# A searched order with an offset for each kind of operation, and scores of the global queries taken over each key once

## The chip, the cores and the metric

The kernel runs on 1 core of one Trainium2 chip. The metric is the device time of one execution in microseconds, in the median of several runs. A profiled execution has a time of its own and, a little shorter, a span from its first to its last instruction; stretches and sums below are of that span.

## The reference

Three stages follow each other, for 4 batches of 576 tokens. The first is an attention of 8 heads in which 32 global queries see all 544 keys, and 512 local queries see the 32 global keys and the local keys at a distance of at most 32. The second is a causal attention with 4 experts, of which a gate picks two for each token. The third is a convolution of three taps with a gate.

```python
s_g = scale * q_g @ concat(k_g, k_l).T          # 32 x 544, every key once
out_g = softmax(s_g) @ concat(v_g, v_l)
out_l = softmax(concat(q_l @ k_g.T, band(q_l @ k_l.T, 32))) @ concat(v_g, v_l)
x = concat(out_g, out_l) as (B, 544, 512)
logits = x @ w_gate; w = softmax over the two largest
out = sum over experts e: w_e * (causal_softmax(x@wq[e], x@wk[e]) @ (x@wv[e])) @ wo[e]
h = relu(out @ w_in); y = (h * sigmoid(conv3(h))) @ w_out
```

The second stage works on 544 tokens here, with inputs in float32; `w_in` is folded with `wo` into one matrix before it is used.

## The kernel before

The work is divided into some 1,900 operations (`op`), each a small group of instructions of one engine with a tag, for example `scoresA` (TensorE) or `expA` (ScalarE). The program doesn't issue them in the order in which it is written. `Schedule.run` places them one after the other: on each engine, among the operations whose inputs are ready, it takes the one with the smallest priority `prio`. A priority is a due time: `at(kind, b, f)` sets it from the table `PLAN` (stage A, B or C of batch b, and the weights' stages F, U, W) and the fractions in `SUB`. `HOLD` is added on TensorE to the priority of an operation that needs the array in another tile shape than the last, `HORIZON` says how far ahead of the earliest open due time an operation may be taken, and `CAPS` how many buffers of a kind may live at once. All engines then run their instructions in the order that came out, and SyncE (SP) issues all loads and stores in its order; a later instruction of an engine never passes an earlier one that waits.

Stage A of a batch (`stage_a`) treats two head pairs at a time. `local` does one head pair: masked scores on TensorE with the array in tiles of 64x32 (L550, L558; tag `scoresA`, 64 records), their maximum on VectorE (L561), 8 exponentials on ScalarE (L567), 8 transposes (L574, array whole) with a copy after each four (L576), the product with V in tiles of 128x32 (L587), its normalisation on VectorE (L594 to L596), 4 transposes (L604), and the copy into the buffer X, as a rounded part on ScalarE (L606) and a rest on VectorE (L361). `glob` does the 32 global queries of two head pairs: scores (L618), maximum (L622), one exponential (L624), 6 transposes (L633), product with V (L646), one transpose (L666), copies into X (L681). The keys are laid out in 24 blocks of 32 (`key_blocks`), in which the global keys stand six times, so that each local query block finds its keys in one run of 128; the global queries' scores run over 22 of the blocks, 704 columns, and `zG` clears the repeated blocks afterwards.

Stage B (`stage_b`) needs all of X of a batch: projections L708 (q, k) and L728 (v and gate), then for each of four query tiles i scores in tiles of 64x128 (L788, L793; two head pairs), exponentials (L800), transposes (L806), the product with V (L816 or L824) and a transpose (L837). Stage C is L919 (first matrix) and L957 (second), 12 matmuls each, 32 and 64 such blocks, with relu, convolution and gate between them on ScalarE, VectorE and GpSimd. The weights are prepared on the chip: `split_weights` (L432, L358), `decode` of `w_in` and `w_out` (L460 to L470), and `fold` (L493, L494), 8 blocks. Result blocks leave by L961 on ScalarE and the store L963.

Of the kernel before, what the change touches and what calls it, by code (L numbers as in the profile page):

```python
# [148 lines left out]
class Schedule:  # L149
# [1 line left out]
    LAT = {"PE": 0.04, "ACT": 0.055, "DVE": 0.055, "POOL": 0.05, "SP": 0.0}  # L151
    TAIL = {"PE": 0.17, "ACT": 0.1, "DVE": 0.06, "POOL": 0.03}
    SWITCH = 0.15
    SLACK = 0.063
    HOLD = 0.47
    HORIZON = 56.132
    RATE = 415e3
    SHARED = {"wi", "wu", "guard", "gate", "cv", "gt", "scB", "cwc"}

    def __init__(self):  # L160
# [3 lines left out]
    def op(self, eng, dur, fn, r=(), w=(), g=(), mode=None, size=0, lead=0.0, tag=""):  # L164
        o = Op()
        o.eng, o.dur, o.fn, o.mode, o.size, o.tag = eng, dur, fn, mode, size, tag
        o.prio = self.prio - lead
        o.port = "DVE" if eng == "POOL" else "POOL" if eng == "DVE" and tag in self.SHARED else None
        o.n = len(self.ops)
        o.succ, o.wait, o.ready = [], 0, 0.0  # L170
        before, bufs = {}, {}
        for t in r:
            wr, rd = self.last.setdefault(t, ([], []))
            before.update(dict.fromkeys(wr))
        for t in w:
            wr, rd = self.last.setdefault(t, ([], []))
            before.update(dict.fromkeys(wr))
            before.update(dict.fromkeys(rd))
        for t in g:
            wr, rd = self.last.setdefault(t, ([], []))  # L180
            before.update(dict.fromkeys(wr))
            before.update(dict.fromkeys(rd))
        for t in w:
            self.last[t] = ([o], [])
        for t in r:
            if t not in w:
                self.last[t][1].append(o)
        for t in tuple(r) + tuple(w):
            b = t[0] if isinstance(t, tuple) else t
            if isinstance(b, Buf):  # L190
                bufs[b] = 1
        o.bufs = tuple(bufs)
        for b in bufs:
            b.left += 1
        for p in before:
            p.succ.append(o)
            o.wait += 1
        self.ops.append(o)
        return o

    def run(self, trace=None):
# [8 lines left out]
        while left:  # L210
# [48 lines left out]
            elif o.eng == "SP":  # L259
                free["SP"] = t + 0.45  # L260
                dma = max(dma, t + 1.6) + o.size / self.RATE
                end = dma + 0.9
            else:
                if o.port:
                    t = max(t, port[o.port])
# [32 lines left out]
def t_pool(n, two=False):  # L298
    return (200 + (2.1 if two else 1.05) * n) * 1e-3


PLAN = {"A": [(-9.1, 23.2), (27.9, 79.0), (79.4, 165.8), (164.7, 245.1)],
        "B": [(34.0, 82.4), (87.3, 167.4), (178.8, 261.8), (257.7, 331.7)],
        "C": [(92.3, 184.6), (173.0, 288.4), (267.5, 353.2), (351.8, 398.6)],
        "F": (29.4, 53.5),
        "U": (62.9, 102.6),
        "W": (18.7, 72.1)}


CAPS = dict(raw=1, t=2, p=2, P=6, PT=2, PU=5, hb=4, cv=3, Pg=1, PGT=1)  # L310

MEM = (13, 9, 3, 4, 14)

SUB = {"lk": 15.574, "lv": 8.685, "ly": 7.388, "lw": 9.802, "ag": 0.054, "az": 0.179, "bq": 0.033, "bp": 0.145, "bv0": 0.113,
       "bv": 0.03, "bg": 0.301, "b0": 0.264, "b1": 0.436, "b2": 0.674, "b3": 0.738, "bl": 0.688, "bs": 0.012, "ch": 0.08,
       "co": 0.252, "cm": 0.179, "cf": 0.034, "cz": 0.549, "pi": 0.0, "pu": 0.0}


@with_exitstack
def body(ctx, tc, kq, vA, wqv, woT, w_in, conv_w, w_out, cmask, out, trace=None,  # L320
# [221 lines left out]
    def local(b, kb, v0, v1, X):  # L542
# [63 lines left out]
        op("ACT", t_act(512, 1), lambda: act.activation(X.ap()[:, 32:S], tx.ap(), AF.Copy), r=[tx], w=[(X, "h")], tag="xh")  # L606
        op("DVE", t_dve(512), lambda: sub(X.ap()[:, S + 32:2 * S], tx.ap(), X.ap()[:, 32:S]), r=[tx, (X, "h")], w=[(X, "l")], tag="xl")

    def glob(b, u, kqs, vs, X):
        G = PB(2, 3)  # L610

        def scores():
            for a, e in ((0, 512), (512, 704)):
                for z in range(2):
                    for y in range(2):
                        rows = slice(64 * y, 64 * y + 64)
                        c = 2 * z + y
                        pe.matmul(G.ap()[32 * c:32 * c + 32, a:e], kqs[z].ap()[rows, KB + 512:KB + 544], kqs[z].ap()[rows, a:e],  # L618
                                  start=True, stop=True)
        op("PE", 1.17, scores, r=[kqs[0], kqs[1]], w=[G], mode="64x32", tag="scoresG")  # L620
        st, Pg, PGT = ST(), W(2, 4, "Pg"), W(2, 0, "PGT")
        op("DVE", t_dve(704), lambda: dve.tensor_reduce(st.ap()[:, 0:1], G.ap()[:, :704], axis=AX.X, op=ALU.max, negate=True), r=[G], w=[st], tag="maxG")  # L622
        op("POOL", .25, lambda: scale_pool(st.ap()[:, 1:2], st.ap()[:, 0:1], 0.125), r=[st], w=[(st, 1)], tag="sclG")
        op("ACT", t_act(704, 1, 1), lambda: act.activation(Pg.ap()[:, :704], G.ap()[:, :704], AF.Exp, bias=st.ap()[:, 1:2], scale=0.125),  # L624
           r=[G, (st, 1)], w=[Pg], tag="expG")
        op("POOL", .2, lambda: pool.memset(Pg.ap()[:, 128:768].rearrange("p (a c) -> p a c", a=5)[:, :, 0:32], 0.0), w=[Pg], tag="zG")
        op("POOL", .15, lambda: pool.memset(Pg.ap()[:, 704:768], 0.0), w=[(Pg, 1)], g=[G], tag="zG")
        tp = PB(2, 1)

        def trans():  # L630
            for m in range(6):
                sl = slice(128 * m, 128 * m + 128)
                pe.transpose(tp.ap()[:, sl], Pg.ap()[:, sl], ident)  # L633
        op("PE", .65, trans, r=[Pg, (Pg, 1)], w=[tp], mode="f", tag="transG")
        op("ACT", t_act(768, 1), lambda: act.activation(PGT.ap()[:, :768], tp.ap()[:, :768], AF.Copy), r=[tp], w=[PGT], tag="ptG")
        o = PB(1, 0)

# [419 lines left out]
```

## Time and profile before

| | |
|---|---|
| time, 3 runs | median 453.15 us (450.85 to 453.31) |
| profiled execution | 452.34 us |
| its span | 450.2 us |
| mean granted clock of TensorE, as a share of full speed | 0.99 |
| TensorE busy | 423.6 us (94%) |
| VectorE, ScalarE, GpSimd busy | 274.1, 248.6, 106.0 us |
| loads and stores | 43.09 MB |

Busy shares are of the whole span. A share of 94% on TensorE says that its order and its idle stretches decide the time, and that the other engines matter where TensorE waits for them.

### The profile page before, as it was taken

What the parts mean: (1) busy time and instruction counts of PE and PEld (TensorE: products, weight loads), DVE (VectorE), ACT (ScalarE), POOL (GpSimd) and SP (SyncE); (2) the same over time, 40 slices, a digit from 0 to 9 for tenths busy, and PEclk for the clock granted to TensorE, in tenths of its full rate; (3) what the DMA queues carried; (4) which work ended last, traced back from release to release, by engine and by line L of the source; (5) the groups of instructions that cost most, each with busy time, mean ns of one, the idle gap of its engine ahead of it and who ended that gap; (6) DMA issues with size and microseconds to landing.
All of it is one profiled execution on the core that took longest, in us unless ns stands there. A gap on an engine that the chain in (4) does not pass through costs nothing.

```text
span 450.2 us, 15387 instructions
## 1 busy us (share of the span) xinstructions
PE 423.6 (94%) x6692; PEld 372.8 (83%) x6692; DVE 274.1 (61%) x580; ACT 248.6 (55%) x563; POOL 106.0 (24%) x262
## 2 busy tenths in 40 slices
PE   5768999988989999989999999999999999999995
PEld 2645568966869998978899998987999999899995
DVE  1366886778766566268654755269365722876871
ACT  3854565459865555567655444668343535644551
POOL 2232143752450140010210240020033200213410
PEclk9979999999999999999999999999999999999998
DMA  8995854526320510342010500000000010001011
GB/s 310 395 385 173 305 160 182 184 69 238 104 97 4 198 42 1 108 155 94 14 50 27 206 2 26 1 28 3 3 1 26 2 51 26 1 3 51 1 52 50
DMA packets 15171, 43.09 MB, mean 96 GB/s; under 512 B 1536, under 2 KB 6400, under 8 KB 15104
## 3 DMA queue, kind: packets, MB, share of 16 engines
q1 hardware_dynamic: 15104, 42.12, 26.7%
q8 instruction: 52, 0.85, 0.8%
q14 instruction: 15, 0.12, 0.1%
HBM read 37.65 MB, written 4.46 MB: 94 GB/s over the span
## 4 chain that ended last, share of the span: by engine, by line
PE 87%; ACT 4%; DVE 3%; issue 3%; DMA 2%; POOL 0%; SPq 0%; ACTq 0%; DVEq 0%
PE acc L957 22%; PE acc L708 11%; PE acc L919 11%; PE acc L728 7%; PE acc L788 4%; PE acc L806 4%; PE acc L824 4%; PE acc L493 4%; PE acc L587 3%; PE acc L574 3%; PE acc L558 3%; PE acc L618 2%; PE acc L604 2%; DMA kq<-in_kq_dram 2%; PE acc L859 1%
## 5 line engine op out<-in xcount | busy, mean ns | idle before, releaser
L957 PE MATMUL acc<-xg,wuh 128*128 128x272 f32 x512 | 100.9, 294 | 0.3 <-ACT work L926 0.3
L957 PEld LDWEIGHTS acc<-xg,wuh 128*128 128x128 f32 x512 | 79.7, 188 | 2.0 <-issue 0.6
L934 DVE SCALAR_TENSOR_TENSOR work<-work,cw 128x272 f32<-128x272 f32 x128 | 64.7, 536 | 19.7 <-POOL work L355 19.5
L957 PE MATMUL acc<-xg,wul 128*128 128x272 f32 x256 | 73.5, 287 | 0.0
L355 POOL TENSOR_SCALAR work<-work,cw 128x272 f32<-128x272 f32 x64 | 34.9, 558 | 100.1 <-ACT work L926 81.2
L919 PE MATMUL acc<-o,wfh 128*128 128x274 f32 x256 | 51.5, 296 | 0.1
L708 PE MATMUL acc<-xg,wqvh 128*128 128x272 f32 x256 | 49.6, 291 | 0.0
L957 PEld LDWEIGHTS acc<-xg,wul 128*128 128x128 f32 x256 | 48.1, 188 | 0.0
L567 ACT ACTIVATE work<-acc,st 128x128 f32<-128x128 f32 x128 | 35.2, 385 | 19.3 <-POOL st L355 16.5
L919 PEld LDWEIGHTS acc<-o,wfh 128*128 128x128 f32 x256 | 40.2, 189 | 1.3 <-DVE o L361 0.5
L708 PEld LDWEIGHTS acc<-xg,wqvh 128*128 128x128 f32 x256 | 40.0, 188 | 0.7 <-issue 0.4
L800 ACT ACTIVATE work<-acc,st 128x128 f32<-128x128 f32 (+3 forms) x64 | 30.7, 529 | 15.2 <-DVE st L796 9.5
L796 DVE TENSOR_REDUCE st<-acc 128x2 f32<-128x256 f32 (+3 forms) x32 | 26.3, 821 | 19.5 <-PE acc L793 18.7
L919 PE MATMUL acc<-o,wfl 128*128 128x274 f32 x128 | 37.1, 290 | 0.0
L708 PE MATMUL acc<-xg,wqvl 128*128 128x272 f32 x128 | 36.8, 287 | 0.0
L938 ACT ACTIVATE work<-work 128x544 f32<-128x544 f32 x32 | 21.2, 661 | 20.3 <-DVE work L934 20.2
L728 PE MATMUL acc<-wqvh,xg 128*128 128x260 f32 (+1 forms) x160 | 32.1, 288 | 0.0
L561 DVE TENSOR_REDUCE st<-acc 128x8 f32<-128x1024 f32 x16 | 19.6, 1224 | 19.9 <-PE acc L558 18.7
L939 DVE SCALAR_TENSOR_TENSOR work<-work 128x544 f32<-128x544 f32 x32 | 23.1, 723 | 13.0 <-ACT work L938 12.7
L808 ACT ACTIVATE work<-acc 128x128 f32<-128x128 f32 (+3 forms) x64 | 24.7, 441 | 6.6 <-PE acc L806 5.8
L361 DVE TENSOR_TENSOR xg<-work,xg 128x544 fp32r<-128x544 f32 x32 | 23.4, 732 | 7.6 <-ACT xg L943 7.5
L926 ACT ACTIVATE work<-acc 128x546 f32<-128x546 f32 x32 | 20.1, 633 | 14.1 <-PE acc L919 10.4
(136 smaller groups left out, 846.0 us busy)
## 6 DMA issues: line engine op xcount, KB each, us to landing
v<-in_vA_dram SPq DMA_DIRECT2D x32, 487.5 KB, 5.3
kq<-in_kq_dram SPq DMA_DIRECT2D x16, 656.0 KB, 4.7
out_dram<-work SPq DMA_DIRECT2D x16, 272.0 KB, 2.2
early<-in_w_in_dram SPq DMA_DIRECT2D x8, 512.0 KB, 9.0
work<-in_w_out_dram SPq DMA_DIRECT2D x8, 512.0 KB, 6.6
early<-in_wqv_dram SPq DMA_DIRECT2D x4, 386.0 KB, 7.0
early<-in_woT_dram SPq DMA_DIRECT2D x1, 512.0 KB, 8.8
cb<-in_cmask_dram SPq DMA_DIRECT2D x1, 232.0 KB, 2.6
```

Source lines behind the costliest of these rows:

```text
L355: pool.tensor_scalar(dst, src, s, 1.0, op0=ALU.mult, op1=ALU.mult)
L361: dve.tensor_tensor(lo, src, hi.bitcast(F32), op=ALU.subtract)
L567: op("ACT", t_act(128, 1, 1), lambda y=y, t=t, sl=sl: act.activation(P[y].ap()[:, sl], S_(y)[:, sl], AF.Exp, bias=st.ap()[:, 8 + 4 * y + t ...
L708: pe.matmul(acc.ap()[:, 512 * z:512 * z + 272], wa[:, c, m], xa[:, s], start=(n == 0), stop=(n == 11))
L728: pe.matmul(acc.ap()[:r, :260], x[:, o_ + 128 * i:o_ + 128 * i + r], wa[:, c, :], start=(n == 0), stop=(n == 11))
L796: op("DVE", t_dve(2 * w), lambda t=t, st=st: dve.tensor_reduce(st.ap()[:, 0:2], t.ap().rearrange("p (y c) -> p y c", y=2)[:, :, :w], axis= ...
L800: op("ACT", t_act(w, 1, 1), lambda t=t, st=st, y=y, Pb=Pb: act.activation(Pb.ap()[:, :w], t.ap()[:, 512 * y:512 * y + w], AF.Exp, bias=st. ...
L808: op("ACT", t_act(w, 1), lambda PT=PT, tp=tp: act.activation(PT.ap()[:, :w], tp.ap()[:, :w], AF.Copy), r=[tp], w=[PT], tag="ptB")
L919: pe.matmul(acc.ap()[:, 512 * f:512 * f + 274], a[:, p, sl], O[:, x, p, 270 * z:270 * z + 274], start=(k == 0), stop=(k == 5))
L934: op("DVE", t_dve(272, 1), lambda hv=hv, cvv=cvv, f=f, F=F, z=z, k=k, o_=o_: dve.scalar_tensor_tensor(cvv()[:, f], hv()[:, f, o_ + z:o_ + ...
L939: op("DVE", t_dve(544, 1), lambda hv=hv, cvv=cvv, z=z: dve.scalar_tensor_tensor(cvv(), cvv(), 1.0, hv()[:, :, 1 + z:1 + z + N], op0=ALU.ad ...
L957: pe.matmul(acc.ap()[:, 512 * m:512 * m + N], w[:, F, sl], G.ap()[:, o_ + N * f:o_ + N * f + N], start=(F == 0 and k == 0), stop=(F == 7 a ...
```

## The change

There are two parts. The first is the order. Every number of the tables is another: due times in `PLAN`, fractions in `SUB`, `HOLD` from 0.47 to 9.121, `HORIZON`, and nearly no limits in `CAPS`. A new table `OFF` adds an amount to the due time of each kind of operation, by its tag. And where the scheduler places a load or a store after the first 5 us, it takes its end 1.1 us later than before.

The second is in `glob`. The global queries' scores are taken over each key once: 480 columns (five runs of 96 local keys), and 64 (the global keys and the last 32 local ones), 544 in place of 704. The exponential that read 704 columns becomes two that write their results to the same places of the buffer as before; the repeated blocks are cleared as before, but the clearing only waits for the exponentials to have been read from the scores' buffer.

```diff
     SWITCH = 0.15
-    SLACK = 0.063
-    HOLD = 0.47
-    HORIZON = 56.132
+    SLACK = 0.07
+    HOLD = 9.121
+    HORIZON = 72.7
+    OFF = {'amask': -3.9, 'cmask': -8.0, 'cv': 25.2, 'cv1': 0.5, 'cw': 1.6, 'epsA': 1.8, 'epsG': 25.2, 'epsL': -7.7, 'expA': -0.4, 'expB': 22.7, 'expG': 6.5, 'expL': -10.1, 'fold': 1.4, 'gate': -2.7, 'gh': 15.5, 'gl': 7.2, 'glast': 9.0, 'h': 1.6, 'kq': 18.2, 'lg': 2.6, 'maxB': 1.8, 'maxG': 1.0, 'maxL': -0.3, 'nrmA': -4.7, 'nrmB': 5.7, 'nrmG': 3.4, 'oh': 1.0, 'ol': 4.0, 'oll': 2.4, 'one': -8.6, 'out': 0.3, 'projQK': 6.6, 'projV': 1.0, 'ptA': 17.0, 'ptB': 1.1, 'ptG': 3.6, 'pvA': -8.3, 'pvB': 0.6, 'pvG': 17.0, 'pvL': 28.8, 'pvW': 0.8, 'qkh': 2.9, 'qkl': 1.2, 'ql': 2.2, 'recA': 3.5, 'recB': -16.8, 'recG': -0.6, 'recL': -2.7, 'relu': -6.8, 'sclA': -0.5, 'sclG': -13.1, 'scoresA': 1.3, 'scoresG': -2.7, 'scoresL': -4.3, 'store': -1.2, 'tanh': -3.9, 'transA': -0.5, 'transB': -3.3, 'transG': -0.8, 'transL': -14.0, 'transO': -12.5, 'transOL': -2.6, 'transX': 5.9, 'transXG': -2.0, 'v': 19.9, 'wfh': -6.5, 'wfl': -4.4, 'wi': -5.4, 'wo': 2.6, 'woh': -5.6, 'wqkl': 1.8, 'wqv': 7.4, 'wqvh': 15.4, 'wu': -5.8, 'wuh': -4.9, 'wul': 1.0, 'wvl': -0.2, 'xgh': -0.3, 'xgl': -2.3, 'xh': -0.1, 'xl': 19.1, 'y': -2.0, 'zG': 2.7, 'zL': -8.7, 'zh': -18.2}
...
-        o.prio = self.prio - lead
+        o.prio = self.prio - lead + self.OFF.get(tag, 0.0)
...
-                end = dma + 0.9
+                end = dma + (0.9 if dma < 5 else 2.0)
...
-PLAN = {"A": [(-9.1, 23.2), (27.9, 79.0), (79.4, 165.8), (164.7, 245.1)],
...
+PLAN = {"A": [(-30.9, 33.4), (23.8, 79.3), (69.8, 161.6), (164.2, 217.9)],
...
-CAPS = dict(raw=1, t=2, p=2, P=6, PT=2, PU=5, hb=4, cv=3, Pg=1, PGT=1)
+CAPS = dict(raw=1, t=19, p=8, P=4, PT=48, PU=6, hb=13, cv=6, Pg=26, PGT=11)
...
-SUB = {"lk": 15.574, "lv": 8.685, "ly": 7.388, "lw": 9.802, "ag": 0.054, "az": 0.179, "bq": 0.033, "bp": 0.145, "bv0": 0.113,
+SUB = {"lk": 14.883, "lv": -0.851, "ly": -0.447, "lw": 0.255, "ag": -0.07, "az": 0.204, "bq": -0.041, "bp": 0.341, "bv0": 0.152,
...
+    def keys(k, n, w, at_, step):
+        if n == 5:
+            return k[:, :640].rearrange("p (n c) -> p n c", n=n)[:, :, at_:at_ + w]
+        return k[:, :1312].rearrange("p (n c) -> p n c", c=32)[:, 0:22:21]
+
     def glob(b, u, kqs, vs, X):
         G = PB(2, 3)
 
         def scores():
-            for a, e in ((0, 512), (512, 704)):
+            for (a, e), (n, w, at_, step) in (((32, 512), (5, 96, 32, 128)), ((512, 576), (2, 32, 0, 672))):
                 for z in range(2):
                     for y in range(2):
                         rows = slice(64 * y, 64 * y + 64)
                         c = 2 * z + y
-                        pe.matmul(G.ap()[32 * c:32 * c + 32, a:e], kqs[z].ap()[rows, KB + 512:KB + 544], kqs[z].ap()[rows, a:e],
-                                  start=True, stop=True)
-        op("PE", 1.17, scores, r=[kqs[0], kqs[1]], w=[G], mode="64x32", tag="scoresG")
+                        pe.matmul(G.ap()[32 * c:32 * c + 32, a:e], kqs[z].ap()[rows, KB + 512:KB + 544],
+                                  keys(kqs[z].ap()[rows], n, w, at_, step), start=True, stop=True)
+        op("PE", .95, scores, r=[kqs[0], kqs[1]], w=[G], mode="64x32", tag="scoresG")
         st, Pg, PGT = ST(), W(2, 4, "Pg"), W(2, 0, "PGT")
-        op("DVE", t_dve(704), lambda: dve.tensor_reduce(st.ap()[:, 0:1], G.ap()[:, :704], axis=AX.X, op=ALU.max, negate=True), r=[G], w=[st], tag="maxG")
+        op("DVE", t_dve(544), lambda: dve.tensor_reduce(st.ap()[:, 0:1], G.ap()[:, 32:576], axis=AX.X, op=ALU.max, negate=True), r=[G], w=[st], tag="maxG")
         op("POOL", .25, lambda: scale_pool(st.ap()[:, 1:2], st.ap()[:, 0:1], 0.125), r=[st], w=[(st, 1)], tag="sclG")
-        op("ACT", t_act(704, 1, 1), lambda: act.activation(Pg.ap()[:, :704], G.ap()[:, :704], AF.Exp, bias=st.ap()[:, 1:2], scale=0.125),
-           r=[G, (st, 1)], w=[Pg], tag="expG")
-        op("POOL", .2, lambda: pool.memset(Pg.ap()[:, 128:768].rearrange("p (a c) -> p a c", a=5)[:, :, 0:32], 0.0), w=[Pg], tag="zG")
+        op("ACT", t_act(480, 1, 1), lambda: act.activation(Pg.ap()[:, :640].rearrange("p (n c) -> p n c", n=5)[:, :, 32:128],
+           G.ap()[:, 32:512].rearrange("p (n c) -> p n c", n=5), AF.Exp, bias=st.ap()[:, 1:2], scale=0.125), r=[G, (st, 1)], w=[(Pg, 0)], tag="expG")
+        op("ACT", t_act(64, 1, 1), lambda: act.activation(Pg.ap()[:, :704].rearrange("p (n c) -> p n c", c=32)[:, 0:22:21],
+           G.ap()[:, 512:576].rearrange("p (n c) -> p n c", n=2), AF.Exp, bias=st.ap()[:, 1:2], scale=0.125), r=[G, (st, 1)], w=[(Pg, 2)], tag="expG")
+        op("POOL", .2, lambda: pool.memset(Pg.ap()[:, 128:768].rearrange("p (a c) -> p a c", a=5)[:, :, 0:32], 0.0), w=[(Pg, 3)], g=[G], tag="zG")
         op("POOL", .15, lambda: pool.memset(Pg.ap()[:, 704:768], 0.0), w=[(Pg, 1)], g=[G], tag="zG")
         tp = PB(2, 1)
 
...
-        op("PE", .65, trans, r=[Pg, (Pg, 1)], w=[tp], mode="f", tag="transG")
+        op("PE", .65, trans, r=[(Pg, k) for k in range(4)], w=[tp], mode="f", tag="transG")
```

Line numbers of the changed kernel are higher by 1 up to the function `keys`, and by 8 behind the scores of `glob`. The number of TensorE operations is the same; only their order differs, at many places. Three of them bear on the time.

The first is on TensorE about 20 to 40 us into the program, where the last local blocks of batch 0 are worked on. Before, these rows stood in a row: a masked score block (L558), a product with V, transposes, a block of `fold` (L493, L494), and then the global scores (L618).

```order
L558 MATMUL acc<-kq 32x128 x32
L587 MATMUL acc<-v,work 32x65 x32
L604 MATMUL acc<-ident,work 128x128 x4
L574 MATMUL acc<-ident,work 128x128 x8
L493 MATMUL acc<-early 128x512
L494 MATMUL acc<-xg,o 128x512
L493 MATMUL acc<-early 128x512
L494 MATMUL acc<-xg,o 128x512
L618 MATMUL acc<-kq 32x512 x4
L618 MATMUL acc<-kq 32x192 x4
```

In the changed kernel the same part of the program on TensorE reads as follows. L559, L575, L588, L605 are the lines that were L558, L574, L587, L604; L641, L654 and L674 were L633, L646 and L666; L624 are the global scores.

```order
L559 MATMUL acc<-kq 32x128 x32
L641 MATMUL acc<-ident,work 128x128 x6
L575 MATMUL acc<-ident,work 128x128 x8
L588 MATMUL acc<-v,work 32x65 x32
L575 MATMUL acc<-ident,work 128x128 x8
L588 MATMUL acc<-v,work 32x65 x32
L654 MATMUL acc<-v,work 32x65 x24
L605 MATMUL acc<-ident,work 128x128 x4
L624 MATMUL acc<-kq 32x480 x4
L624 MATMUL acc<-kq 32x64 x4
L674 MATMUL acc<-ident,work 128x128
L605 MATMUL acc<-ident,work 128x128 x4
```

No block of `fold` stands there any more. One more local score block follows, and then at once the projections of batch 0 (L736 and L716), 13 blocks of 12 matmuls with a `transG`, a product with V and a `transX` between them. All 8 blocks of `fold` now stand behind the projections, among the query tiles of stage B of batch 0; before, all 8 stood ahead of the first projection. Counted up to the first projection, TensorE has 6 local score blocks, 3 blocks of global scores, 40 transposes of `transA`, 12 of `transG`, 16 of `transX`, 2 of `transXG`, 4 products `pvA` and 2 `pvG` in the changed kernel. ScalarE has, up to the last copy into X that this projection needs, 40 exponentials of local blocks, 2 pairs of global ones, 10 copies L577, 2 copies L643, 4 copies L607, 6 small copies L689, 4 roundings L433, one L479, and 4 operations L461 of `decode`. On SP the loads of V for the second half of batch 0 stand behind three loads of `w_in`, one of `wqv` and one of `w_out`.

The second place is where TensorE goes to another tile shape. As an example, the end of the first score block of batch 3 in stage B, before: its mask rows (L793), and then a block of stage C (L919).

```order
L793 MATMUL acc<-cb 128x64
L793 LDWEIGHTS cb
L793 MATMUL acc<-cb 128x64
L919 MATMUL acc<-o,wfh 128x274 x2
L919 MATMUL acc<-o,wfl 128x274
```

In the changed kernel the mask rows of the same block are L801, and the second head pair's score block (L796) stands right behind it.

```order
L801 MATMUL acc<-cb 128x64
L801 LDWEIGHTS cb
L801 MATMUL acc<-cb 128x64
L796 MATMUL acc<-k,q 128x128 x6
L801 LDWEIGHTS cb
L801 MATMUL acc<-cb 128x128
```

Blocks of one shape stand side by side more often. Counted over all of TensorE's operations, the shape changes 155 times before and 132 times after the change; the array goes back to its whole shape 68 times before and 57 times after.

The third place is the end of the program on ScalarE. Before, the last two rows are the copies of the last two result blocks, shown here with the counters that each waits for; the DMA counters are taken in turn by the loads and stores, and DMAHW6 is that of the store just ahead of the last.

```order
L938 ACTIVATE work<-work 128x544 [waits DVE_49,Pool_49]
L943 ACTIVATE xg<-work 128x544 [waits DVE_49,PE_49]
L961 ACTIVATE work<-acc 128x544 [waits PE_49]
L961 ACTIVATE work<-acc 128x544 [waits DMAHW6_49,PE_49,Activation_49]
```

In the changed kernel the last copy (L969) waits for DMAHW5, the store ahead of that one, which belongs to a block whose matmuls stand eight blocks of 12 ahead of the end.

```order
L946 ACTIVATE work<-work 128x544 [waits DVE_49]
L951 ACTIVATE xg<-work 128x544 [waits DVE_49,PE_49]
L969 ACTIVATE work<-acc 128x544 [waits PE_49,Pool_49]
L969 ACTIVATE work<-acc 128x544 [waits DMAHW5_49,PE_49]
```

The buffer of the last result is now one that an older store has read.

## Rows read from the trace of the kernel before

**Rows 1.** The page, first part: busy time of each engine.

```profile
PE 423.6 (94%) x6692; PEld 372.8 (83%) x6692; DVE 274.1 (61%) x580; ACT 248.6 (55%) x563; POOL 106.0 (24%) x262
```

**Rows 2.** Busy time of TensorE by stretch: length, busy, granted clock, DMA.

```profile
0.00:60.00 60.00, 45.89 (x907) 0.94 0.83 303
90.00:110.00 20.00, 16.93 (x413) 1.00 0.40 128
110.00:440.00 330.00, 325.74 (x4968) 1.00 0.15 50
```

**Rows 3.** The same view in stretches of 4 us, around the low clock.

```profile
24.00:28.00 4.00, 1.15 (x12) 0.98 1.02 410
28.00:32.00 4.00, 3.17 (x7) 0.50 1.03 418
32.00:36.00 4.00, 4.00 (x29) 0.67 0.41 135
```

**Rows 4.** Timeline of TensorE: start, length, line, shapes, count.

```profile
5.34 1.96 PE L558 MATMUL acc<-kq 64*32 64x128 f32 x64 [1.33 <-DMA kq<-in_kq_dram]
...
61.94 1.04 PE L574 MATMUL acc<-ident,work 128*128 128x128 f32 x8
62.91 0.41 PE L550 MATMUL acc<-cb 64*32 64x512 bf16 x8
...
64.19 1.11 PE L587 MATMUL acc<-v,work 128*32 128x65 f32 x64
65.24 0.33 PE L666 MATMUL acc<-ident,work 128*128 128x128 f32 x1
```

**Rows 5.** Timeline of ScalarE, with idle time before a row in brackets.

```profile
8.96 2.17 ACT L567 ACTIVATE work<-acc,st 128x128 f32<-128x128 f32 x8 [6.94 <-POOL st L355]
12.59 0.85 ACT L624 ACTIVATE work<-acc,st 128x704 f32<-128x704 f32 x1
14.80 0.81 ACT L635 ACTIVATE work<-acc 128x768 f32<-128x768 f32 x1
18.11 0.85 ACT L432 ACTIVATE wqvh<-early 128x772 fp32r<-128x772 f32 x1 [0.28 <-DMA early<-in_wqv_dram]
18.87 0.58 ACT L606 ACTIVATE xg<-acc 128x512 fp32r<-128x512 f32 x1
19.34 1.08 ACT L576 ACTIVATE work<-acc 128x512 f32<-128x512 f32 x2
20.87 0.66 ACT L460 ACTIVATE early<-early 128x512 f32<-128x512 f32 x1
```

**Rows 6.** Groups by line and shape: global scores, count, then busy us and mean ns.

```profile
L618 PE MATMUL acc<-kq 64*32 64x512 f32 x64 | 11.2, 656 | 0.7 <-DVE o L361 0.5 <-DMA kq<-in_kq_dram 0.2
L618 PE MATMUL acc<-kq 64*32 64x192 f32 x64 | 4.9, 335 | 0.0
```

**Rows 7.** The chain that ended last: start, length, what.

```profile
51.69 1.32 PE acc L618 x16
...
349.42 1.50 PE acc L957 x12
...
355.23 1.71 PE acc L957 x12
```

**Rows 8.** Timeline of TensorE where a block of scores begins.

```profile
346.54 0.41 PE L708 MATMUL acc<-xg,wqvh 128*128 128x272 f32 x2
346.80 0.29 PE L708 MATMUL acc<-xg,wqvl 128*128 128x272 f32 x1
347.01 0.55 PE L788 MATMUL acc<-k,q 64*128 64x128 f32 x6
```

**Rows 9.** Timeline of the end, TensorE and ScalarE.

```profile
444.75 0.28 PE L957 MATMUL acc<-xg,wul 128*128 128x272 f32 x1
443.56 0.63 ACT L961 ACTIVATE work<-acc 128x544 f32<-128x544 f32 x1 [3.11 <-PE acc L957]
446.53 0.62 ACT L961 ACTIVATE work<-acc 128x544 f32<-128x544 f32 x1 [2.34 <-DMA out_dram<-work]
```

More of the change, by code (lines that the diff above doesn't have):

```diff
@@ L299, in t_pool @@
     return (200 + (2.1 if two else 1.05) * n) * 1e-3
-PLAN = {"A": [(-9.1, 23.2), (27.9, 79.0), (79.4, 165.8), (164.7, 245.1)],
[L303 to L307, printed above, removed]
-CAPS = dict(raw=1, t=2, p=2, P=6, PT=2, PU=5, hb=4, cv=3, Pg=1, PGT=1)
+PLAN = {"A": [(-30.9, 33.4), (23.8, 79.3), (69.8, 161.6), (164.2, 217.9)],
+        "B": [(11.0, 76.3), (72.6, 160.5), (172.6, 263.2), (261.3, 315.1)],
+        "C": [(87.9, 142.4), (185.3, 282.3), (260.8, 349.4), (375.6, 480.7)],
+        "F": (42.7, 78.3),
+        "U": (53.4, 128.5),
+        "W": (12.9, 58.1)}
+CAPS = dict(raw=1, t=19, p=8, P=4, PT=48, PU=6, hb=13, cv=6, Pg=26, PGT=11)
 MEM = (13, 9, 3, 4, 14)
-SUB = {"lk": 15.574, "lv": 8.685, "ly": 7.388, "lw": 9.802, "ag": 0.054, "az": 0.179, "bq": 0.033, "bp": 0.145, "bv0": 0.113,
-       "bv": 0.03, "bg": 0.301, "b0": 0.264, "b1": 0.436, "b2": 0.674, "b3": 0.738, "bl": 0.688, "bs": 0.012, "ch": 0.08,
-       "co": 0.252, "cm": 0.179, "cf": 0.034, "cz": 0.549, "pi": 0.0, "pu": 0.0}
+SUB = {"lk": 14.883, "lv": -0.851, "ly": -0.447, "lw": 0.255, "ag": -0.07, "az": 0.204, "bq": -0.041, "bp": 0.341, "bv0": 0.152,
+       "bv": 0.041, "bg": 0.673, "b0": 0.303, "b1": 0.441, "b2": 0.741, "b3": 0.864, "bl": 0.651, "bs": 0.012, "ch": 0.079,
+       "co": 0.411, "cm": 0.301, "cf": 0.089, "cz": 0.634, "pi": 0.0, "pu": 0.0}
 @with_exitstack
```

## The prediction

> **What bounds the kernel now.** I read the page first: TensorE is busy for 423.6 of 450.2 us [rows 1], so at most 26.6 us can come from idle time, and the rest only from less work on TensorE. Then I read where this idle time lies, by stretches. From 0 to 60 us 14.1 us are idle (60 - 45.89), from 90 to 110 us 3.1 (20 - 16.93), and in the 330 us from 110 to 440 only 4.3 (330 - 325.74) [rows 2]; 60 to 90 us has none, and the last 5.2 us are the end, when the last results go out. [...] So the reader is to look at three things: how the first 60 us are filled, what a block on TensorE costs, and the end.
>
> **The sum, against the profiled execution's own 452.34 us (span 450.2, and 2.14 around it).**
>
> Global scores. 704 columns become 544, in 8 blocks of 16 records. One block took 1.32 us [rows 7]. By columns alone that is 160/704 of it, 0.30 us. The two shapes say a little less: 656 ns for 512 columns and 335 for 192 [rows 6] make 1.0 ns a column above a fixed part, so that 480 and 64 columns would take 624 and 207, 16% less for the pair, 0.21 us a block. Eight blocks: 1.7 to 2.4 us, all on TensorE. The new columns are read in five runs of 96, which no row shows; were that slower than one run, the gain could be 0, and that is the lower bound. I take 2.0, since both shapes that the rows show cost by the column.
>
> The exponential in two. ScalarE has 8 more instructions. In the trace eight exponentials of 128 columns stand in 2.17 us [rows 5], 0.27 us each, so a piece of 64 columns adds about 0.2 us, 1.6 us in all on an engine that is busy for 55% [rows 1]. It is hidden by that idle time in all but the two blocks of the first 40 us, where I count it in the sum below; without cover it would cost 1.6. [...]
>
> Changes of tile shape. A block of stage C in a row of its kind took 1.50 us, and 1.71 where a block of scores in another shape stood ahead of it [rows 7], 0.21 for the way back to the whole array. On the way out, starts within a block stand 0.13 apart (346.54 to 346.80 for two) and the first of the scores came 0.21 behind the last, 0.08 more [rows 8]. A pair of changes costs 0.29 us. TensorE goes back to the whole array 57 times in place of 68, so 11 x 0.29 = 3.2 us less. Bounds: 0, if TensorE waits there anyway; twice that, if other pairs of shapes cost more. 44 of the 68 lie behind the first block of stage C, where TensorE hardly ever waits [rows 2], and 30 of the 57; so I take 3.2.
>
> The end. The last copy on ScalarE began at 446.53, after a wait of 2.34 for a store that still read its buffer; its matmuls had ended at 445.03 (444.75 and 0.28) [rows 9]. After the change it waits for a store whose block ends eight blocks of 1.50 us earlier. So it begins at 445.05: 1.5 us less, and what follows it, copy and store, is as long as before. Bounds: 0 and 1.5.
>
> The first 60 us. The projections of batch 0 need all of X of that batch, and in the changed order `fold` no longer fills the time until then, so I ask which engine is late. ScalarE's rows up to the last copy into X: 40 exponentials in fives of 2.17 (10.9), ten copies in pairs of 1.08 (5.4), two of 0.81 (1.6), four of 0.58 (2.3), four roundings of 0.85 (3.4), four of `decode` of 0.66 (2.6), two global exponentials of 0.85 and 0.2 more each (2.1) [rows 5], and, as an estimate from these rows' widths, 2 us for one wide rounding and six small copies. That is 30.3 us from 8.96 on without a pause: 39.3, and the projections begin at about 40 us. TensorE's work up to there: 70 transposes at 0.12 (8 from 61.94 to 62.91), 6 local score blocks at 1.28, 4 products at 1.05 and 2 of three quarters of that [rows 4], 3 global blocks at 1.1: 8.4 + 7.7 + 4.2 + 1.6 + 3.3 = 25.2 us. So 14.8 of the first 40 us are lost, and behind them stand 13 blocks of projections whose inputs are there, with nothing lost up to 60 us. Before, the loss by 60 us was 14.1 idle, and about 2.9 by the low clock (1.6 of the 3.17 busy us from 28 to 32, and a third of 4 from 32 to 36) [rows 2, 3], and the slow start: the first local block took 1.96 us where it later takes 1.28 less its masks, about 1.06 [rows 4], and with the global block behind it I put that at 2.2. Together 19.2. The 14.8 has the slow start in it. If the clock falls again (2.9), the gain is 1.5; if not, 4.4. With 25.2 us of work in 40 TensorE is about as thinly used ahead of the projections as before, so I take that it falls: 1.5. What could make it worse is a load that ScalarE waits for, and a longer stay at the low clock; I bound that side by a second fall, a loss of 1.4.
>
> Stage B of batch 0. There 3.1 us were idle from 90 to 110 us [rows 2], with query tiles and little else for TensorE. The 8 blocks of `fold` now lie between these tiles, so what waited for the gate and the exponentials has cover; but their decoding goes to VectorE and ScalarE at the same time. I take half of it, 1.5 us less, with bounds of 3.1 less and, below, more.
>
> From 110 to 440 us I leave the 4.3 us as they are. Sum: 2.0 + 3.2 + 1.5 + 1.5 + 1.5 = 9.7, so 442.6 us against 452.34. The median shown is 0.8 above that execution, which would make 443.4; the lowest run is 1.5 below it. I predict 442.5.
>
> **Rivals.**
>
> Decoding stalls stage B. `w_in` and `w_out` are decoded while the tiles of batch 0 run. If the whole of that stretch, some 50 us, idles as 90 to 110 did (3.1 in 20), it loses 7.7 us in place of 1.6: 448.6. For it: VectorE's and ScalarE's work per us of TensorE is highest there. Against it: `fold` itself is 8 blocks that need little of either. Chance 0.15.
>
> No fall of the clock, and stage B without idle time. 442.5 less 2.9 and 1.6: 438, or a little under if the counted changes cost more. Against it: the thin stretch is still there. Chance 0.13.
>
> The change doesn't do what it says: runs of 96 columns are as slow as 704 in one, and changes of shape lie where TensorE waits anyway. Then 2.0 and 3.2 are gone: 447.8, and with half of the gains in the first 110 us gone too, 449.3 to 451.5. Chance 0.09, half of it within 0.5% of before.
>
> Slower: the clock stays low under the projections. [...] For it: 14.8 lost us ahead of the projections, in many short pieces. Against it: before, the clock was back within 8 us, once TensorE worked without a pause [rows 3]. [...] Chance 0.05.
>
> **How the numbers follow.** The forecast and its near surroundings (438.5 to 447) have 0.58. The range should leave out 2 in 10: 436 at its low end (all bounds on the good side make 452.34 - 2.4 - 4.5 - 1.5 - 4.4 - 3.1 = 436.4), and 451 at its high end, which takes in the stalled stage B and most of the third rival. About 0.5% (2.3 us) is what a measurement of this kernel can tell from no change. Faster by more than that, under 450.9: 0.58 + 0.13 + 0.15 less a tail of 0.02, half of the third rival, 0.88, which I cut to 0.84, since an order that is changed in every place can wait in places that I haven't read. Within: 0.10. Slower: 0.06.
>
> **What would show it.** The first projection (L736) at 38 to 42 us, and TensorE without a pause for 20 us from there; a granted clock of 0.5 for 5 to 8 us somewhere from 26 to 42. Blocks of L624 that take 1.0 to 1.1 us. TensorE's busy time lower by 4 to 6 us, idle time from 110 to 440 us still 3 to 6. No wait for a store ahead of the last L969. The prediction is wrong if idle time from 60 to 110 us is over 6, or if from 110 to 440 it is over 8.

## The result

The changed kernel takes 440.68 us (median of 4 runs, 439.35 to 440.71) where the kernel before takes 452.69 (450.85 to 453.31): a ratio of 0.973, 95% interval 0.970 to 0.977. It was predicted at 442.5, in a range of 436 to 451. (The head of this document speaks of 576 tokens a batch; it is 544.) Times below are medians of 4 to 12 runs; one run of 1388 us, of the old order with halved loads, stands far outside the other eleven (451.0 to 454.6) and is left out of the ratio there. The kernel before was run again beside each set of experiments (452.19, 451.96 and 452.94 us), the changed kernel was not, so a difference of under 1 us to its 440.68 means little.

The page of the changed kernel, first part, and then TensorE's busy time by stretch (length, busy, granted clock, DMA), the last stretch being the end:

```profile
PE 415.9 (95%) x6692; PEld 373.9 (85%) x6692; DVE 268.5 (61%) x578; ACT 247.9 (57%) x569; POOL 107.0 (24%) x262
```

```profile
0.00:60.00 60.00, 46.75 (x1068) 0.94 0.83 315
60.00:110.00 50.00, 47.83 (x661) 1.00 0.33 118
110.00:430.00 320.00, 316.53 (x4946) 1.00 0.16 55
430.00:438.50 8.50, 4.78 (x39) 1.00 0.19 66
```

The span is 438.5 us, 11.7 less than before. TensorE's busy time fell by 7.7 (423.6 to 415.9, [rows 1]) and its idle time by 4.0 (26.6 to 22.6). Beside [rows 2], idle time in the first 60 us is 13.25 (14.11 before), behind 110 us about 0.8 less, and at the end 3.7.

The end went as foreseen. ScalarE's last two rows on its timeline, against [rows 9]: no store holds the last copy.

```profile
433.37 0.63 ACT L969 ACTIVATE work<-acc 128x544 f32<-128x544 f32 x1 [4.65 <-PE acc L965]
434.82 0.62 ACT L969 ACTIVATE work<-acc 128x544 f32<-128x544 f32 x1 [0.82 <-PE acc L965]
```

The head did not. TensorE's timeline from 20 us on (start, length, line, shapes, the count of matmuls behind the x):

```profile
20.13 0.48 PE L654 MATMUL acc<-v,work 128*32 128x65 f32 x18 [1.54 <-issue]
20.40 0.23 PE L588 MATMUL acc<-v,work 128*32 128x65 f32 x2
20.41 0.25 PE L654 MATMUL acc<-v,work 128*32 128x65 f32 x2
20.45 1.12 PE L588 MATMUL acc<-v,work 128*32 128x65 f32 x62
21.60 0.33 PE L674 MATMUL acc<-ident,work 128*128 128x128 f32 x1
21.77 1.04 PE L575 MATMUL acc<-ident,work 128*128 128x128 f32 x8
22.73 1.12 PE L624 MATMUL acc<-kq 64*32 64x480 f32 x16
23.79 0.66 PE L605 MATMUL acc<-ident,work 128*128 128x128 f32 x4
24.56 0.41 PE L551 MATMUL acc<-cb 64*32 64x512 bf16 x8
24.78 0.40 PE L559 MATMUL acc<-kq 64*32 64x128 f32 x7
26.33 0.98 PE L559 MATMUL acc<-kq 64*32 64x128 f32 x53 [1.15 <-issue]
...
32.25 0.27 PE L559 MATMUL acc<-kq 64*32 64x128 f32 x1 [3.76 <-issue]
...
46.34 0.39 PE L736 MATMUL acc<-wqvh,xg 128*128 128x260 f32 x1
```

Three stalls, 6.45 us in all (1.54, 1.15 and 3.76), wait for nothing that the profile shows ("issue"), and each breaks a block in the middle. Add the counts from the first stall to the second: 18 + 2 + 2 + 62 + 1 + 8 + 16 + 4 + 8 + 7 = 128 matmuls, so with their weight loads 256 instructions. From the second to the third it is 128 again. Instructions are also on the DMA queues: the page has "q8 instruction: 52" pieces of 16 KB for TensorE's 13,384: about 257 to a piece, so about 64 bytes each. Here are the DMA queues in three stretches of 0.2 us, which begin at 17.6, 23.7 and 29.8 us (packets, MB, share of 16 engines): in each a piece is under way, beside loads that fill the engines.

```profile
q1 hardware_dynamic: 15, 0.08, 92.1%
q8 instruction: 1, 0.02, 31.7%
...
q1 hardware_dynamic: 17, 0.07, 79.8%
q8 instruction: 1, 0.02, 33.6%
...
q1 hardware_dynamic: 25, 0.09, 110.0%
q8 instruction: 1, 0.02, 35.2%
```

A piece takes 1.0 to 1.1 us of one engine. TensorE goes on 1.3 to 1.5 us after it is there (at 18.7, 24.8 and 31.0 us), and the next piece starts 3.5 to 3.7 us after that. So my theory from here on: **TensorE's instructions come in pieces of 256, one ahead, and a piece queues behind the loads**; with the DMA full (397 to 418 GB/s from 16 to 36 us) it comes every 6.1 us, and blocks of small tiles, 128 matmuls in 2.2 us between the second stall and the third, run dry. The kernel before has the same, with 0.61, 2.19 and 0.66 us, the first two 128 matmuls apart and the third 256 behind; I had read over it.

```profile
16.18 0.43 PE L587 MATMUL acc<-v,work 128*32 128x65 f32 x16 [0.61 <-issue]
...
22.38 0.63 PE L558 MATMUL acc<-kq 64*32 64x128 f32 x21 [2.19 <-issue]
...
39.55 0.70 PE L493 MATMUL acc<-early 128*128 128x512 f32 x1 [0.66 <-issue]
```

### The profile page after: what moved, and what is told of

It is laid out like the page before. It is cut to its first block, busy times and chain, and to the rows that moved or that the text cites. A ratio compares the mean times of both kernels' runs of the same rounds, so it can differ in the third digit from the quotient of the medians.

```text
span 438.5 us, 15375 instructions
## 1 busy us (share of the span) xinstructions
PE 415.9 (95%) x6692; PEld 373.9 (85%) x6692; DVE 268.5 (61%) x578; ACT 247.9 (57%) x569; POOL 107.0 (24%) x262
## 4 chain that ended last, share of the span: by engine, by line
PE 91%; ACT 3%; issue 2%; DVE 2%; DMA 1%; POOL 0%; SPq 0%; DVEq 0%; POOLq 0%; ACTq 0%
PE acc L965 23%; PE acc L927 11%; PE acc L716 11%; PE acc L736 7%; PE acc L796 4%; PE acc L814 4%; PE acc L832 4%; PE acc L588 4%; PE acc L559 3%; PE acc L494 3%; PE acc L575 3%; PE acc L624 2%; PE acc L605 2%; PE acc L867 1%; PE acc L641 1%
## 5 line engine op out<-in xcount | busy, mean ns | idle before, releaser
L356 POOL TENSOR_SCALAR work<-work,cw 128x272 f32<-128x272 f32 x64 | 33.8, 540 | 66.6 <-ACT work L934 58.2
L716 PE MATMUL acc<-xg,wqvh 128*128 128x272 f32 x256 | 49.8, 292 | 0.0
L808 ACT ACTIVATE work<-acc,st 128x128 f32<-128x128 f32 (+3 forms) x64 | 30.2, 528 | 21.7 <-DVE st L804 16.8
L716 PEld LDWEIGHTS acc<-xg,wqvh 128*128 128x128 f32 x256 | 39.8, 188 | 0.2
L716 PE MATMUL acc<-xg,wqvl 128*128 128x272 f32 x128 | 36.7, 287 | 0.0
L736 PE MATMUL acc<-wqvh,xg 128*128 128x260 f32 (+1 forms) x160 | 32.5, 288 | 0.1
L562 DVE TENSOR_REDUCE st<-acc 128x8 f32<-128x1024 f32 x16 | 19.6, 1224 | 19.1 <-PE acc L559 17.6
L951 ACT ACTIVATE xg<-work 128x544 fp32r<-128x544 f32 x32 | 21.1, 658 | 13.3 <-DVE work L947 10.9
```

Source lines behind the costliest of these rows:

```text
L356: pool.tensor_scalar(dst, src, s, 1.0, op0=ALU.mult, op1=ALU.mult)
L716: pe.matmul(acc.ap()[:, 512 * z:512 * z + 272], wa[:, c, m], xa[:, s], start=(n == 0), stop=(n == 11))
L736: pe.matmul(acc.ap()[:r, :260], x[:, o_ + 128 * i:o_ + 128 * i + r], wa[:, c, :], start=(n == 0), stop=(n == 11))
L808: op("ACT", t_act(w, 1, 1), lambda t=t, st=st, y=y, Pb=Pb: act.activation(Pb.ap()[:, :w], t.ap()[:, 512 * y:512 * y + w], AF.Exp, bias=st. ...
```

## The experiments

**The columns, in either order.** Two kernels: the new order with the old scores, and the old order with the new ones.

```diff
 # new order, old scores; the old order got the reverse, with the exponential in two
-            for (a, e), (n, w, at_, step) in (((32, 512), (5, 96, 32, 128)), ((512, 576), (2, 32, 0, 672))):
+            for a, e in ((0, 512), (512, 704)):
```

> The changed kernel with the global scores over 704 columns again (scores and their maximum; the two exponentials read the same 544 of them), every instruction in the new order. The prediction's term of 2.0 us for the columns (0.21 to 0.30 us a block, eight blocks) gives 440.7 + 2.0 = 442.7 us, L624 blocks of 1.3 to 1.4 us at full clock and the first block longer by 0.9 us or more, since it ran at half clock. Rival: the columns were paid for by idle time of TensorE, so that the whole gain is the order's: 440.7 us, busy time higher and idle time lower by the same 2 us.

> The kernel before with the global scores over each key once (544 columns) and the exponential in two, every instruction in the old order. If the columns lie on the path: 452.7 - 2.0 = 450.7 us, and if the second exponential costs what it can at most (0.2 us eight times), 452.3 us. Rival: what the columns free on TensorE turns into idle time before the transposes, 452.7 us with the same busy time less 2 us and idle time more by 2 us. Any gain far over 2.4 us would say that the columns, not the order, carry the change.

The first took 442.88 us (442.16 to 443.68), 2.2 more than the changed kernel; the second 452.14 beside 452.19 for the kernel before, ratio 1.001 (0.998 to 1.004). In the new order the columns are worth what was forecast; in the old one the time shows nothing. Where the traces of the changed kernel and of the first are laid over each other matmul by matmul, each block behind the first 60 us starts what follows it 0.24 to 0.27 us sooner in the changed kernel, inside the forecast 0.21 to 0.30. In the head the two are 0.3 us apart from the first keys on, before any score; 2.0 us apart behind the second block, most of it because with the old scores the granted clock was 0.57 from 20 to 24 us where the changed kernel has 1.00; and 0.3 us again behind the third stall for instructions. So the head keeps nothing of its first two blocks. The first block, expected to be 0.9 us longer because of a half clock, was 0.14 longer (2.60 beside 2.46); in the changed kernel, where it takes 2.46 us and the second block 1.12, the granted clock is 1.00 from 4 to 12 us.

That the columns are worth nothing in the old order is not shown. The profiled run of the second kernel had a granted clock of 0.50 from 24 to 36 us and 0.81 from 36 to 40, more of the lower level than [rows 3], and its twelve runs have a mean clock of 0.987 in the middle where the 29 of the kernel before have 0.990. At 0.987 and 0.988 its six runs have a median of 450.9 us, the five of the kernel before 452.7. The clock may have taken what the columns gave; why it was low for longer, no run tells.

The first kernel is also the new order by itself: 9.3 us under the kernel before, ratio 0.981 (0.977 to 0.986). The first part of its page:

```profile
PE 419.0 (95%) x6692; PEld 375.0 (85%) x6692; DVE 269.6 (61%) x578; ACT 247.8 (56%) x569; POOL 106.3 (24%) x262
```

**The last copy.**

```diff
-                y = W(1, 0)
+                y = Buf(K_) if (b, z, mp) == (NB - 1, 1, 1) else W(1, 0)
```

> The kernel before with one buffer changed: the very last copy out of PSUM writes to a free buffer of the keys and so waits for no store; nothing else moves. The prediction's term for the end: 452.7 - 1.5 = 451.2 us, the last copy then waits for TensorE alone. Rival: the copy could not have begun earlier anyway, because TensorE's last projection ends as late, 452.7 us.

450.77 beside 452.19 us: 1.4 less, ratio 0.998 (0.995 to 1.001). The interval holds no change, so the time alone doesn't settle it; the row does. ScalarE's last copy, against 2.34 us for the store in [rows 9]:

```profile
446.22 0.62 ACT L961 ACTIVATE kq<-acc 128x544 f32<-128x544 f32 x1 [0.88 <-PE acc L957]
```

**Changes of tile shape, and a control.** In the changed kernel's finished order, a block of the whole array is put ahead of the small block before it, where nothing that it needs or overwrites lies between.

```diff
-        for o in order:
+        for o in regroup(order, True):    # scores, scores, out -> scores, out, scores
+        for o in regroup(order, False):   # (the control) out, scores, out -> out, out, scores
```

> The changed kernel with ten blocks of the whole array put between two blocks of the same smaller tile shape behind 80 us (152 changes of tile shape where it has 132, 67 of them back to the whole array where it has 57); the same instructions otherwise. By the prediction's price of 0.29 us a pair: 440.7 + 2.9 = 443.6 us, as busy or idle time on TensorE beside those ten places. Rival: a change of shape costs nothing in the dense part, 440.7 us, and the gain of the order has to come from the waits and from the clock.

> The control to the ten split pairs, which cost 10.3 us where 2.9 were expected. In the changed kernel seven blocks of the whole array are again put ahead of one small block, but each small block stood between two blocks of the whole array and still does: 132 changes of tile shape, as in the changed kernel, and the same instructions. If the 10.3 us were the price of the changes of shape alone (about 1 us a pair): 440.7 us here. If they came from small blocks that stand 0.8 to 1.6 us later, with the softmax steps behind them late as well (0.4 us of new waits a place in the split kernel): 440.7 + 7 x 0.4 = 443.5 us, as idle time on TensorE ended by ScalarE or VectorE.

The ten split pairs took 450.97 us, 10.3 more than the changed kernel. The control, seven moves without one more change of shape, took 447.75: 7.1 more. So both expectations were too low, and a move costs about 1.0 us with a change of shape or without one. TensorE's busy time from 60 us to the end, in the changed kernel, the ten split pairs and the control, in this order:

```profile
60.00:438.50 378.50, 369.14 (x5627) 1.00 0.19 64
```

```profile
60.00:449.51 389.51, 375.39 (x5637) 1.00 0.18 62
```

```profile
60.00:446.46 386.46, 371.16 (x5638) 1.00 0.19 63
```

The ten pairs add 6.25 us of busy time and 4.8 of idle time; the control adds 2.0 and 5.9. In both profiled runs the first projection came 1.2 to 1.3 us later, ahead of any move (the granted clock over the first 60 us was 0.91, for 0.94 in the changed kernel), so about that much work came behind 60 us. That leaves some 5 us of busy time for ten pairs, 0.5 a pair, and 0.8 for seven moves of the control, 0.1 a move. The price of a pair, over that of a move, is then about 0.4 us in place of 0.29. This is an estimate: it comes from busy time in two kernels whose moves stand at different places. The waits that are new in the control, by who waits for whom:

```profile
PE acc L605 <- DVE gw L754: 1.5, 1, 1.5
PE acc L845 <- DVE work L839: 1.5, 2, 1.2
PE acc L605 <- DVE work L597: 1.3, 1, 1.3
PE acc L814 <- ACT work L808: 1.3, 1, 1.3
PE acc L716 <- DVE work L839: 1.2, 1, 1.2
```

A small block that stands one block later lets what VectorE or ScalarE makes of its result (L597, L808, L839) come late, and the transposes and projections behind it wait. In this kernel a place in the order is worth more than a change of shape.

**Do loads hold up the instructions?** Copies from memory to memory are issued where the DMA is quiet and TensorE runs small blocks.

```diff
+            if o.eng == "ACT" and 2080 < done < 2560 and made < 20:   # done: matmuls so far
+                turn += 1
+                if turn % 2:
+                    act.dma_start(extra[made, :, :1024], w_out[128 * (made % 8):128 * (made % 8) + 128].bitcast(F32))   # control: 16 columns
+                    made += 1
```

> The changed kernel with 16 copies of 512 KB from one place of the memory to another, issued by ScalarE's queue between about 130 and 150 us, where the transfers are otherwise light; everything else as it was. First theory: TensorE's instructions come in pieces of 256 (128 matmuls and 128 weight loads), one is asked for when the one before is entered, and under full transfers it takes 6.1 us instead of about 3; pieces are entered at 135.6, 137.7, 144.7 and 148.0 us, so that 3 to 6 us of stalls without a releaser appear there: 444 to 447 us. Rival: the stalls of the first 35 us belong to places of the program (its first run through the instructions, or the half clock), and transfers have no part in them: 440.7 us and no new stall without a releaser.

> The control to the extra copies: the same 16 issues on ScalarE's queue at the same places, of 64 bytes a row instead of 4096 (8 KB each). If the bytes on the way count: 440.7 us and no new stall on TensorE. If ScalarE's issuing is what costs: the same time as with the large copies.

(There are 12 copies; the 16 of the two texts is a miscount.) 449.36 us with the large copies (448.19 to 450.74), 441.76 with the small ones (440.18 to 442.30). On TensorE's timeline from 130 to 155 us the rows with a stall for instructions (the changed kernel has one of 1.14 us here already) are, with the large copies,

```profile
139.89 1.09 PE L832 MATMUL acc<-vB,work 128*32 128x65 f32 x58 [1.91 <-issue]
153.75 1.49 PE L559 MATMUL acc<-kq 64*32 64x128 f32 x34 [4.53 <-issue]
```

and with the small ones

```profile
148.77 0.84 PE L559 MATMUL acc<-kq 64*32 64x128 f32 x34 [1.24 <-issue]
```

TensorE's busy time in this stretch, first with the large copies, then with the small:

```profile
130.00:155.00 25.00, 18.56 (x475) 0.95 0.87 286
```

```profile
130.00:155.00 25.00, 23.13 (x518) 1.00 0.31 94
```

Idle time is 6.44 us in place of 1.87. The stalls stand at two of the four places that the forecast named, and most of the rest of the 7.6 us is the clock: after the pause of 4.53 us, 34 matmuls take 1.49 us where they took 0.84 (the granted clock is 0.57 from 152 to 160 us), 2.5 us until the two traces run alike. So transfers hold up instructions, with a price of their own and one through the clock, and the stalls are not tied to the start of the program.

**Can the head be relieved?** Each large load is cut in two by columns; then in two and in four with the first two loads whole.

```diff
-        op("SP", 0.08, lambda: sp.dma_start(view(), src), w=[(buf, key) if key is not None else buf],
+            for i in range(2):
+                at_, e = 4 * (c * i // 8), c if i == 1 else 4 * (c * (i + 1) // 8)
+                sp.dma_start(v[:, at_:e], src[:, at_:e])
```

> The changed kernel with each load of keys, values and weights cut in two by columns: the same bytes in rows half as long (packets of about 2 KB instead of 4 KB), the same order on every engine. A piece of instructions waits about 3.7 us behind the loads before it starts. If it waits behind a number of packets, that falls to about 1.9 us and the three stalls of 6.45 us in the first 35 us fall to 2 us or less: 436 to 437 us. If it waits behind a number of bytes: 440.7 us, stalls as before. If the loads themselves become slower by their shorter rows or by twice as many issues (0.35 to 0.5 us each on the load queue, where 512 KB take 1.3 us): stalls on loads appear and the time is over 441 us.

> The changed kernel with the loads cut in two by columns, but the first two loads of keys whole: in the run with all loads halved the first keys landed 1.8 us later (the first scores began at 7.17 us, not 5.34). If that lateness stays on the path to the end: 438.5 - 1.8 = 436.7 us, with stalls of TensorE's instructions of 2 to 3 us in all. Rival: the stalls and ScalarE's sums take up what the start gains: 438.5 us.

> The same with the loads cut in four (packets of about 1 KB), the first two whole. If a piece of instructions waits behind a number of packets, it now waits under 1 us and no stall of instructions is left before 40 us: 434.5 to 436 us. Rival: a load of 512 KB now takes four issues of 0.35 to 0.5 us, 1.4 to 2 us where its bytes take 1.3 us, so that the loads come later and TensorE waits for them: 437 us or more. Second rival: the wait is for bytes, and the halved loads helped by their slower issue alone: stalls of instructions as with halves.

Halved, 438.47 us (436.56 to 438.55); halved but for the first two, **437.20 us** (436.47 to 438.89), ratio to the kernel before 0.967 (0.963 to 0.970), the lowest median, though the range of the one lies within that of the other; quartered, 459.34. TensorE's first keys and its one stall for instructions in the first 45 us, all loads halved:

```profile
7.17 1.96 PE L567 MATMUL acc<-kq 64*32 64x128 f32 x64 [3.20 <-DMA kq<-in_kq_dram]
...
30.48 0.41 PE L567 MATMUL acc<-kq 64*32 64x128 f32 x3 [2.33 <-issue]
```

One stall of 2.33 us in place of 6.45. Pieces now come every 5.0 to 5.5 us instead of 6.1 (5 from 12 to 36 us, for 4 in the changed kernel), not in half the time. The first keys came 1.83 us later, and still the first projection began 1.5 us sooner than in the changed kernel (44.83): what lies between is 3.3 us shorter for 4.1 us less of stalls. With the first loads whole, the stalls are 0.41, 0.95 and 4.14 us, 0.95 less than in the changed kernel, and the first projection begins 0.84 sooner. In both runs the rest of the gain sits behind 110 us, where two further stalls of the changed kernel fall away, 1.0 us at the first and 1.3 at the second:

```profile
116.77 0.70 PE L832 MATMUL acc<-vB,work 128*32 128x65 f32 x33 [0.81 <-issue]
...
147.99 0.84 PE L559 MATMUL acc<-kq 64*32 64x128 f32 x34 [1.14 <-issue]
```

So the time that was expected with the first loads whole (436.7) came near, but not by the way that was forecast: the projections begin 0.7 us later than with all loads halved. Neither packets nor bytes alone explain how long a piece waits, and **that stays open**. In quarters, the three large stalls are gone, and TensorE waits for the loads themselves:

```profile
PE acc L633 <- DMA kq<-in_kq_dram: 6.8, 2, 4.5
PE acc L597 <- DMA v<-in_vA_dram: 4.7, 3, 4.0
```

From 12 to 36 us the loads then run at 239 GB/s instead of 407, since the load queue issues without a pause and takes 0.46 to 0.74 us for each quarter (164 KB of keys would need 0.41 at the old rate).

**The kernel before, relieved.** The same halves in the old order, without and with the new scores.

> The kernel before with its loads cut in two by columns, the first three whole; order and arithmetic untouched. Its own stalls without a releaser are 0.61, 2.19 and 0.66 us in the first 40 us. If they set the pace of its first 40 us: 452.2 - 2 to 3 = 449 to 450 us. Rival: its head is bound by ScalarE, VectorE and the half clock, as the prediction had it, and the stalls only take the place of other waits: 452.2 us.

> The kernel before with the loads halved and the global scores over each key once, in the old order. The columns alone gave nothing in the old order (452.1 beside 452.2 us). If the stalls of instructions hid them, they show here: 1.5 to 2.2 us below the kernel before with halved loads alone. Rival: they are hidden by what follows the scores in the old order (the softmax steps on VectorE and ScalarE, or the half clock): no difference between the two.

452.27 and 451.98 us, with 452.94 for the kernel before (ratios 0.999, 0.997 to 1.002, and 0.999, 0.996 to 1.001). Neither run shows the gain that its first theory forecast. But the halves did not relieve the old order, so they don't test whether its stalls set its head. With the old scores its first two stalls were

```profile
16.49 0.43 PE L596 MATMUL acc<-v,work 128*32 128x65 f32 x16 [1.72 <-issue]
...
21.96 0.63 PE L567 MATMUL acc<-kq 64*32 64x128 f32 x21 [1.47 <-issue]
```

in place of 0.61 and 2.19, and the first of them moves by itself: it is 1.58 us in the kernel with the other last buffer, whose head is that of the kernel before. What sets the old order's head stays open. ScalarE's timeline of the run with the new scores shows one candidate, behind the third block's two exponentials:

```profile
55.18 0.32 ACT L642 ACTIVATE work<-acc,st 128x64 f32<-128x64 f32 x1
57.65 0.67 ACT L469 ACTIVATE early<-early 128x512 f32<-128x512 f32 x1 [2.16 <-DMA early<-in_w_in_dram]
58.60 0.85 ACT L441 ACTIVATE wqvh<-early 128x772 fp32r<-128x772 f32 x1 [0.28 <-DMA early<-in_wqv_dram]
59.36 0.79 ACT L655 ACTIVATE work<-acc 128x768 f32<-128x768 f32 x1
```

The exponential ends at 55.5 us, but the copy that the products with V need stands in ScalarE's queue behind a step of `decode` and a rounding that wait for their loads, until 59.36. Scores that come sooner would only lengthen that wait. No run tested this, and the clock, told of above, is a rival to it.

## Why the prediction was right

The sum of 9.7 us met 11.7 (profiled run against profiled run) with two kinds of error that partly cancel: what TensorE has to do fell by more than forecast (7.7 us of busy time, 2.0 and 3.2 in the sum), and the head and stage B gave less (0.9 us each, for 1.5). That the total came this near owes something to luck.

**Global scores (2.0).** Right in the new order: 2.2 us by the medians, 1.5 between the two profiled spans, runs of 96 columns at no extra cost, blocks of 1.05 us from start to start of what follows (1.32 with the old scores), inside the forecast's 1.0 to 1.1. In the old order the time shows nothing, which the prediction didn't foresee; the longer low clock of those runs keeps open whether the columns or something else is the reason.

**The exponential in two.** Right: 668 and 315 ns a pair against 850 in [rows 5], 0.13 us more a block, and no matmul waits for the second one (two weight loads do, 0.3 us together).

**Changes of shape (3.2).** The direction was right, the size too small and the reason too narrow. The order alone took 4.6 us off TensorE's busy time (423.6 before, 419.0 in the new order with the old scores) at nearly the same granted clock (0.990 and 0.988); the split pairs say 0.4 to 0.5 us a pair, which would be 4.4 to 5.5 for eleven. The two agree within what other differences of the orders may hold, but that the 4.6 is the shapes' alone is argued, not shown. And the split pairs and their control together say that a block's place costs more than its shape, a term that the prediction's sum doesn't have. Its low end of 436.4 also took 4.5 us for the shapes, where its own bound (twice 3.2) is 6.4.

**The end (1.5).** Right: 1.42 us by time, 1.46 by the row.

**The first 60 us (1.5).** Idle time by 60 us fell by 0.9, but not by the step that the prediction took. What failed is "without a pause" in ScalarE's sum, which put the projections at 40 us: they began at 46.34. ScalarE's work was well counted: up to the last copy into X, at 44.94, it was busy for 28.8 us, of 30.3 in the sum. But it paused for 7.2 us in that time, and its two longest pauses wait for what TensorE did behind the stalls of 1.54 and 3.76 us:

```profile
21.97 0.56 ACT L689 ACTIVATE xg<-acc 64x32 fp32r<-64x32 f32 x4 [1.30 <-PE acc L674]
...
33.36 0.81 ACT L643 ACTIVATE work<-acc 128x768 f32<-128x768 f32 x1 [3.38 <-PE acc L641]
```

TensorE's stalls for instructions, 6.45 us, are about as much as the projections came late, and the prediction had no term for them. The halved loads bear out that they lie on this path, though they also change when the loads land: there the head is 3.3 us shorter for 4.1 us less of them. The clock fell as forecast: 0.68 from 32 to 36 us, 0.50 from 36 to 40, and 0.96 from 40 to 44. The 64 matmuls of L588 that begin at 35.92 us took 1.96 us, those at 13.54, at 1.00, took 1.11. What it costs was read a little low: five of the 29 runs of the kernel before beside the first experiments kept a granted clock of 0.998 or more and took 447.7 to 449.8 us, the other 24 had 0.992 or less and took 451.4 to 455.3. That is some 4 us, for 2.9 in the prediction; the changed kernel's four runs all had the fall (0.987 to 0.992).

**Stage B of batch 0 (1.5).** From 90 to 110 us TensorE is idle for 1.8 us in place of 3.1, but 0.3 us are new ahead of that: from 60 to 110 us it is 2.2 in place of 3.1, 0.9 less.

**From 110 us on (0).** 0.8 us less, and 1.9 of what is left there are two further stalls for instructions.

Of the checks, the busy time fell by 7.7 us, outside the 4 to 6 (4.6 by the order and 3.1 by the columns, by the new order with the old scores between the two), and L736 was late; the others held, with 19.7 us from 46.34 on without a pause. Of the rivals, decoding stalled nothing (2.2 us idle from 60 to 110), the clock did fall and did come back, and the change did what it says.

## What to carry to other kernels

A stall that breaks a block in the middle and has no releaser is worth a count: if the matmuls between two such stalls, with their weight loads, make 256 instructions, the instructions are likely to be late, and the DMA queues show whether a piece was under way beside full loads. Here smaller loads helped one order (438.47 and 437.20 us beside 440.68) and not the other (452.27 beside 452.94); putting dense runs of small matmuls where few loads run is a thing to try, and no run here tried it. Before a term is priced by its instructions, ask what stands behind it in every queue, and before two orders are compared, look at the granted clock of every run: in the kernel before it moves the time by 4 us.

## What was not expected of the hardware

TensorE's pieces of 256 instructions share the DMA engines with the loads: one came every 6.1 us beside 400 GB/s of loads, and TensorE was idle for 4.6 us more from 130 to 155 us when 12 copies of 512 KB were added there. A pause of 4.5 us cost another 2.5 by the clock behind it (0.57 from 152 to 160 us). Moving seven blocks by one place, with no change of shape, cost 7.1 us.
